# Linear and sliding-window attention in turn: a fourth slot of probabilities, the last tile by head halves, folded first values, and far masks on two engines

## The chip, the cores and the metric

The kernel runs on one core of a Trainium2 chip. The metric is the device time of one execution in microseconds; of the kernel before, three runs gave a median of 434.49 (433.9 to 435.25). The profile was taken on an execution whose span is 432.7 us. Engine names below: PE is TensorE's matmul, PEld its weight load, ACT is ScalarE, DVE is VectorE, POOL is GpSimd, SP is the queue that issues DMAs.

## The reference

Four residual layers on x of 2048 tokens by 512 features, 32 heads of 16: linear attention (A), causal attention in a window of 256 tokens (B), then A and B again with the same weights.

```python
def _A_ref(x, wqkv, wo):                       # linear attention
    q, k, v = split_heads(x @ wqkv)
    phi = lambda t: jnp.where(t > 0, t + 1, jnp.exp(t)) + 1e-6
    pq, pk = phi(q), phi(k)
    kv = jnp.einsum("bhsd,bhse->bhde", pk, v)
    z = jnp.einsum("bhsd->bhd", pk)
    num = jnp.einsum("bhqd,bhde->bhqe", pq, kv)
    den = jnp.einsum("bhqd,bhd->bhq", pq, z)[..., None] + 1e-6
    return merge_heads(num / den) @ wo

def _B_ref(x, wqkv, wo):                       # window W = 256
    q, k, v = split_heads(x @ wqkv)
    scores = jnp.einsum("bhqd,bhkd->bhqk", q, k) * (Dh ** -0.5)
    mask = (idx[:, None] - idx[None, :] >= 0) & (idx[:, None] - idx[None, :] < W)
    p = _softmax(jnp.where(mask[None, None], scores, -1e9), axis=-1)
    return merge_heads(jnp.einsum("bhqk,bhkd->bhqd", p, v)) @ wo

x = x + _A_ref(_layernorm(x), A_wqkv, A_wo)
x = x + _B_ref(_layernorm(x), B_wqkv, B_wo)
x = x + _A_ref(_layernorm(x), A_wqkv, A_wo)
x = x + _B_ref(_layernorm(x), B_wqkv, B_wo)
```

`split_heads` and `merge_heads` stand for the reshapes and transposes of the original.

## The kernel before

The program is written as a list of operations with their reads, writes and PSUM tiles. A table stored in the file fixes beforehand the order of all operations, the engine of those that may go to either ACT or DVE, and the PSUM bank of every tile; semaphores follow from that. Tokens lie in 16 tiles of 128. Excerpts, with cuts marked by `...`; the comments are added here.

```python
# loads, on SP: x in pieces between the first layer's weights
seq += [xs(0, 1), xs(1, 2), xs(2, 4), w("wAk", ...), xs(4, 6), w("wAv", ...)]
seq += [xs(6, 8), w("wAq", ...), xs(8, 12), xs(12, 16)]
...
# layer A: keys, values, queries of a tile; x is normalised and transposed first
def a_k(self, t, key):
    ps = self.tok("k", t, xT, lambda c: K.wA[:, c, 512:1024], ...)     # 4 matmuls, 128x512
    self.phi(ps, lambda: K.pk[:, t, :], ...)        # exp on ACT, min+add and max on DVE
def a_v(self, t, key):
    ps = self.tok("v", t, xT, lambda c: K.wA[:, c, 1024:1536], ...)    # 4 matmuls, 128x512
    self.copy("ve", ps, lambda: K.vA[:, t, :], ...)                    # ACT or DVE
def a_q(self, t, key):
    ps = self.feat("q", t, ...)                                        # 16 matmuls, 128x128
    self.phi(ps, lambda: K.XQ[:, :, t * P:(t + 1) * P], ...)
def a_kv(self, t, kv, z, key):                      # summed over the 16 tiles
    for f in range(4):
        e.matmul(K.ps(kv)[:, fs], K.vA[:, t, fs], K.pk[:, t, fs], ...)
    for f in range(4):
        m = e.matmul(K.ps(z)[:, f:f + 1], K.pk[:, t, fs], K.ones[:, 0:1], ...)
...
# between the keys and the output of a layer A: block mask, product with wo, denominators
self.on("DVE", "kvm", ... K.pqd[:, 0], K.ps(kv), K.bmask ...)
self.pe("M", ... K.pqd[:, 0, f, :], K.wAo[:, f, :] ...); self.copy("Me", ...)
self.pe("den", ...); self.on("DVE", "rec", ... e.reciprocal(K.recf[:], K.ps(ps)[:, 0:P]) ...)
...
def a_out(self, t, key):
    for f in range(4):                              # reciprocals spread over the features
        m = e.matmul(K.ps(ps)[:, f * P:(f + 1) * P], K.spread[:, tg, f, :], K.rec[:, G, :], ...)
    self.on("DVE", "pqd", ... K.pqd[:, s], K.ps(ps), K.XQ[...], ALU.mult ...)
    po = self.tok("aout", t, lambda f: K.pqd[:, s, f, :], lambda f: K.M[:, f, :], ...)
    self.resid(t, po, key + 0.15)
```

Layer B of a tile j of keys: the queries of the next 256 tokens are scored against 64-key blocks b, in four row groups of the array; ACT takes the exponentials into one of three slots of `pb`; DVE multiplies the triangles of the near part (`mk` in b_scores) and of the far part (`mk` in b_far) with a 0/1 mask; the value products of tile j read the slots of tiles j, j-1 and j-2.

```python
def b_scores(self, j, f, key):
    for b in range(2):
        for gq in range(4):
            m = e.matmul(K.ps(ps[gq])[:, 256 * b:256 * b + ns[b]], K.kB[rows, j % 4, 2 * f + b, :, :], K.XQ[rows, f, q:q + ns[b]], ..., tile_position=(32 * gq, 0))
    sl = j % 3
    for h in range(2):
        for b in parts:          # one ACTIVATE of 2x2x256, or two where the window is cut short
            self.on("ACT", "ex", ...)
    self.on("DVE", "mk", ... x, x, K.tri[:, 0, :] ..., ALU.mult ...)       # 128x512
def b_far(self, j, key):
    ...                          # 32 matmuls of 64 columns
    for h in range(2):
        for b in range(2):
            self.on("ACT", "ex", ...)                                      # 128x512
    for b in range(2):
        self.on("DVE", "mk", ... x, x, K.tri[:, 1, :] ..., ALU.mult ...)   # 128x1024
def b_values(self, j, h, key):
    m = e.matmul(K.ps(ps)[:, 34 * u:34 * u + 34], K.pb[:, (b // 2) % 3, gq, f, o:o + P], K.vB[:, (b // 2) % 4, b % 2, r, :], ...)
def b_out(self, j, key, by_pe):
    self.transpose("oT", ...)    # by DMA, of the last tile by PE and one copy
    po = self.tok("bout", j, ...); self.resid(j, po, key + 0.05)
```

The helpers give many operations one line: L351 is `tok` (four matmuls of 512 columns), L365 `feat` (eight of 128 columns), L340 `copy`, L535 and L573 the score matmuls, L549 and L550 the near exponentials (whole and cut), L583 the far ones, L556 and L590 the two masks, L608 the value products, L316 the normalisation, L284 the constant `spread`.

Of the kernel before, what the change touches and what calls it, by code (L numbers as in the profile page):

```python
# [8 lines left out]
ACT = mybir.ActivationFunctionType  # L9
# [14 lines left out]
    same=0.0, pe_first1=5, lat_t=4300, cap_s=8, cap_d=2, cap_e=6, mode=100, sem=35, ring_x=3, wait_s=200,  # L24
# [174 lines left out]


# [5 lines left out]
class Plan:  # L206
# [33 lines left out]
    def load(self, name, emit, nbytes, wr, key):  # L240
        ns = max(500, nbytes / 310)
        return self.on("SP", name, emit, key, (ns, ns + 2400), wr=wr)

    def setup(self):
# [10 lines left out]
        seq += [xs(0, 1), xs(1, 2), xs(2, 4), w("wAk", "wA", "A_wqkv", 512, 1024), xs(4, 6), w("wAv", "wA", "A_wqkv", 1024, 1536)]  # L255
        seq += [xs(6, 8), w("wAq", "wA", "A_wqkv", 0, 512), xs(8, 12), xs(12, 16)]
        seq += [w("wAo", "wAo", "A_wo", 0, 512), w("wBn", "nat", "B_wqkv", 0, 1024)]
        for i, (n, f, b, r) in enumerate(seq):
            self.load(n, f, b, r, key + i if n[0] == "x" or n[:3] in ("wAk", "wAv", "wAq") else 104 + 0.01 * i)
        i = len(seq)  # L260
        self.load("wBv", lambda e: e.dma_start(K.wBv[:], K.B_wqkv.rearrange("(k p) c -> p k c", p=P)[:, :, 1024:1536]), 524288, [("wBv",)], 106)
        self.load("wBo", lambda e: e.dma_start(K.wBo[:], K.B_wo.rearrange("(k p) c -> p k c", p=P)), 524288, [("wBo",)], 107)
# [11 lines left out]

        pool("c3", zero(lambda: K.bmask, 1.0), 151, 200, wr=[("bmask",)])
# [6 lines left out]
        pool("c9", zero(lambda: K.spread), 157, 2000, wr=[("spread",)])  # L282
        for tg in range(4):
            pool("c10", lambda e, tg=tg: e.affine_select(out=K.spread[:, tg, :, :], in_=K.spread[:, tg, :, :], compare_op=ALU.not_equal, fill=1.0, base=-32 * tg, pattern=[[-8, 4], [-1, 8], [0, 16]], channel_multiplier=1), 158, 700, rd=[("spread",)], wr=[("spread",)])  # L284
# [5 lines left out]
        sel = lambda i, base, pat, cm: (lambda e: e.affine_select(out=K.tri[:, i, :], in_=K.tri[:, i, :], compare_op=ALU.is_ge, fill=0.0, base=base, pattern=pat, channel_multiplier=cm))  # L290
        pool("c15", sel(0, 0, [[1, 64]], -1), 162, 200, rd=[("tri",)], wr=[("tri",)])
        pool("c15", sel(1, 64, [[1, 64]], -1), 162, 200, rd=[("tri",)], wr=[("tri",)])
        pool("c15", sel(1, -64, [[0, 64]], 1), 162, 200, rd=[("tri",)], wr=[("tri",)])
        self.on("DVE", "c16", lambda e: e.tensor_tensor(K.tri[:, 0, :], K.tri[:, 0, :], K.tri[:, 1, :], ALU.add), 12, (120, 200), rd=[("tri",)], wr=[("tri",)])
        self.on("DVE", "c16", lambda e: e.tensor_scalar(K.tri[:, 1, :], K.tri[:, 0, :], -1.0, 1.0, op0=ALU.mult, op1=ALU.add), 12, (120, 200), rd=[("tri",)], wr=[("tri",)])
# [13 lines left out]
    def norm(self, t, key, xn_slot, out, wr, by_pe):  # L309

        K = self
        self.on("DVE", "stats", lambda e: e.bn_stats(K.stats[:, t, :], K.xres[:, t, :]), key, dve(512), rd=[("xres", t)], wr=[("stats", t)])  # L312
        self.on("DVE", "aggr", lambda e: e.bn_aggr(K.mv[:, t, :], K.stats[:, t, :]), key + 0.01, (66, 150), rd=[("stats", t)], wr=[("mv", t)])  # L313
        self.on("POOL", "eps", lambda e: e.tensor_scalar(K.ve[:, t, :], K.mv[:, t, 1:2], LN_EPS, None, op0=ALU.add), key + 0.02, (300, 330), rd=[("mv", t)], wr=[("ve", t)])  # L314
        self.on("POOL", "pow", lambda e: e.tensor_tensor(K.rs[:, t, :], K.ve[:, t, :], K.negh[:], ALU.pow), key + 0.03, (640, 690), rd=[("ve", t), ("negh",)], wr=[("rs", t)])  # L315
        self.on("DVE", "xn", lambda e: e.tensor_scalar(K.xn[:, xn_slot, :], K.xres[:, t, :], K.mv[:, t, 0:1], K.rs[:, t, :], op0=ALU.subtract, op1=ALU.mult), key + 0.04, dve(512, "ptr"), rd=[("xres", t), ("mv", t), ("rs", t)], wr=[("xn", xn_slot)])  # L316
        self.transpose("T", lambda: K.xn[:, xn_slot, :], out, [("xn", xn_slot)], wr, key + 0.05, by_pe)
# [66 lines left out]
    def a_v(self, t, key):  # L384
        K = self
        xT = lambda c: K.XQ[:, c, t * P:(t + 1) * P]
        ps = self.tok("v", t, xT, lambda c: K.wA[:, c, 1024:1536], [("XQ", t), ("wAv",)], key)
        self.copy("ve", ps, lambda: K.vA[:, t, :], lambda: K.ps(ps), key + 0.1, 512, wr=[("vA", t)])
# [21 lines left out]
    def layer_a_keys(self, ph, base):  # L410
        self.cls = "E"
        for t in range(T):
            k = 100 * ph + t
            self.norm(t, k - 0.5, t % self.par["ring_x"], lambda t=t: self.XQ[:, :, t * P:(t + 1) * P], [("XQ", t)], t < self.par["pe_first1"])
            self.a_k(t, k)
            self.a_v(t, k + 0.05)
            self.a_q(t, 200 + 4 * (t // 4) + 0.2 * (t % 4) - self.par["k_aq2"])

    def barrier(self, ph):
# [3 lines left out]
        kv, z = Tile(1, "K", False), Tile(1, "K", False)  # L423
        key = 100 * ph + 16
        for t in range(T):
            self.a_kv(t, kv, z, 100 * ph + self.par["k_akv"] + t * 0.001 if late else 100 * ph + t + 0.6)
        key += 2
        if late:
            for t in range(T):
                self.a_q(t, 300 + 4 * (t // 4) + 0.2 * (t % 4) - self.par["k_aq3"])  # L430
        self.on("DVE", "kvm", lambda e: e.tensor_tensor(K.pqd[:, 0, :, :], K.ps(kv).rearrange("p (f n) -> p f n", f=4), K.bmask[:].unsqueeze(1).to_broadcast([P, 4, P]), ALU.mult), key - 2, dve(512), rd=[("bmask",)], wr=[("pqd", 0)], ps=[kv])
        self.on("DVE", "zs", lambda e: e.tensor_tensor(K.zs[:], K.hot[:], K.ps(z)[:, 0:4].unsqueeze(2).to_broadcast([P, 4, 32]), ALU.mult), key - 2, dve(128), rd=[("hot",)], wr=[("zs",)], ps=[z])
        for f in range(4):
            ps = Tile(1, K.cls)
            self.pe("M", lambda e, f=f, ps=ps: e.matmul(K.ps(ps), K.pqd[:, 0, f, :], K.wAo[:, f, :], start=True, stop=True), key - 2 + f * 0.01, 1, 512, rd=[("pqd", 0), ("wAo",)], ps=[ps])
            self.copy("Me", ps, lambda f=f: K.M[:, f, :], lambda ps=ps: K.ps(ps), key - 2 + f * 0.01, 512, wr=[("M", f)])
        for G in range(4):
# [18 lines left out]
            self.g.add("recb", {"ACT": act(128), "DVE": dve(128, "2x")}, lambda e, eng, G=G: e.activation(K.rec[:, G, :], K.recf[:], ACT.Copy) if eng == "ACT" else e.tensor_copy(K.rec[:, G, :], K.recf[:]), k + 0.1, rd=[("recf",)], wr=[("rec", G)])  # L456


    def a_out(self, t, key):
        K = self  # L460
        G, tg = divmod(t, 4)
        ps = Tile(1, K.cls)

        def put(e):
            m = None
            for f in range(4):
                m = e.matmul(K.ps(ps)[:, f * P:(f + 1) * P], K.spread[:, tg, f, :], K.rec[:, G, :], start=True, stop=True)
            return m

        self.pe("spread", put, key, 4, 128, rd=[("rec", G), ("spread",)], ps=[ps])  # L470
        s = t % 2
        self.on("DVE", "pqd", lambda e: e.tensor_tensor(K.pqd[:, s, :, :], K.ps(ps).rearrange("p (f n) -> p f n", f=4), K.XQ[:, :, t * P:(t + 1) * P], ALU.mult), key + 0.05, dve(512), rd=[("XQ", t)], wr=[("pqd", s)], ps=[ps])  # L472
# [404 lines left out]
```

The softmax here doesn't subtract the row's maximum and nothing guards it: scores larger than these inputs give would overflow.

## Time and profile before

| what | value |
|---|---|
| time, median of 3 | 434.49 us |
| span of the profiled execution | 432.7 us |
| PE busy | 402.1 us, 93% |
| DVE busy | 374.7 us, 87% |
| ACT busy | 355.3 us, 82% |
| POOL busy | 83.3 us, 19% |
| near exponentials L549 | 224 of 128x1024, 1050 ns each on average |
| far exponentials L583 | 112 of 128x512, 642 ns |
| far masks L590 | 56 of 128x1024, 678 ns |
| near masks L556 | 128 of 128x512, 415 ns |
| first score of the first layer B | 73.0 us |
| last score of the last layer B | 423.6 us |

Busy time is the union of an engine's instructions, each from its start to its end. Neighbours on one engine overlap, so the mean duration of an instruction is more than the distance from one to the next; for the rate of a stream, read the distance between starts, or a merged piece of the chain divided by its count. PE's ends are modelled, so PE always looks fuller than it is.

### The profile page before, as it was taken

What the parts mean: (1) busy time and instruction counts of PE and PEld (TensorE: products, weight loads), DVE (VectorE), ACT (ScalarE), POOL (GpSimd) and SP (SyncE); (2) the same over time, 40 slices, a digit from 0 to 9 for tenths busy, and PEclk for the clock granted to TensorE, in tenths of its full rate; (3) what the DMA queues carried; (4) which work ended last, traced back from release to release, by engine and by line L of the source; (5) the groups of instructions that cost most, each with busy time, mean ns of one, the idle gap of its engine ahead of it and who ended that gap; (6) DMA issues with size and microseconds to landing.
All of it is one profiled execution on the core that took longest, in us unless ns stands there. A gap on an engine that the chain in (4) does not pass through costs nothing.

```text
span 432.7 us, 17332 instructions
## 1 busy us (share of the span) xinstructions
PE 402.1 (93%) x7576; PEld 265.4 (61%) x7576; DVE 374.7 (87%) x838; ACT 355.3 (82%) x525; POOL 83.3 (19%) x177
## 2 busy tenths in 40 slices
PE   1999999999999999999999999999999999999675
PEld 0555777655665665655656778765667576666443
DVE  5997799999999999988988679999899898987545
ACT  1454546999999999999998443799999999999982
POOL 7789112011120111111000141111000101000000
PEclk9999999999999999999999999999999999999869
DMA  7635104424443555545421000234344443436321
GB/s 241 220 64 148 49 2 106 97 65 97 117 84 82 78 102 101 89 78 107 97 53 26 15 3 2 88 102 102 91 105 94 105 102 101 90 100 101 92 53 51
DMA packets 69292, 37.84 MB, mean 87 GB/s; under 512 B 49248, under 2 KB 64608, under 8 KB 69216
## 3 DMA queue, kind: packets, MB, share of 16 engines
q1 hardware_dynamic: 69216, 36.73, 36.9%
q8 instruction: 60, 0.98, 1.0%
q14 instruction: 16, 0.13, 0.1%
HBM read 6.29 MB, written 2.10 MB: 19 GB/s over the span
## 4 chain that ended last, share of the span: by engine, by line
PE 43%; ACT 41%; DVE 9%; DMA 3%; issue 1%; POOL 1%; SPq 1%; POOLq 0%
ACT pb L549 31%; PE ps L351 19%; PE ps L365 10%; ACT pb L583 7%; PE ps L608 6%; PE ps L535 3%; DMA xres<-in_A_x_dram 2%; ACT pb L550 2%; PE ps L402 1%; DVE stats L312 1%; ACT tE L374 1%; DVE xres L478 1%; DMA xT<-xn 1%; DVE xn L316 1%; PE ps L573 1%
## 5 line engine op out<-in xcount | busy, mean ns | idle before, releaser
L549 ACT ACTIVATE pb<-ps 128x1024 bf16<-128x1024 f32 x224 | 211.1, 1050 | 3.7 <-PE ps L535 2.7
L608 PEld LDWEIGHTS ps<-vB,pb 128*128 128x128 bf16 x2880 | 80.3, 96 | 16.8 <-issue 3.9
L608 PE MATMUL ps<-vB,pb 128*128 128x34 bf16 x2880 | 86.8, 178 | 2.0 <-ACT pb L549 1.0
L314 POOL TENSOR_SCALAR ve<-mv 128x1 f32<-128x1 f32 x64 | 18.1, 283 | 285.3 <-DVE mv L313 284.1
L351 PE MATMUL ps<-wA,XQ 128*128 128x512 bf16 x256 | 65.9, 387 | 3.2 <-DMA wA<-in_A_wqkv_dram 2.8
L365 PE MATMUL ps<-xT,wBp 128*128 128x128 bf16 x1024 | 66.9, 219 | 1.6 <-DVE o L620 0.5
L374 ACT ACTIVATE tE<-ps 128x512 bf16<-128x512 f32 x64 | 38.1, 605 | 35.6 <-PE ps L351 16.9
L365 PEld LDWEIGHTS ps<-xT,wBp 128*128 128x128 bf16 x1024 | 58.2, 98 | 9.5 <-issue 1.7
L583 ACT ACTIVATE pb<-ps 128x512 bf16<-128x512 f32 x112 | 60.8, 642 | 1.6 <-PE ps L573 1.2
L556 DVE TENSOR_TENSOR pb<-pb,tri 128x512 bf16<-128x512 bf16 x128 | 52.2, 415 | 8.6 <-ACT pb L550 4.3
L535 PE MATMUL ps<-XQ,kB 32*128 32x256 bf16 (+3 forms) x1024 | 49.9, 270 | 8.4 <-ACT pb L550 2.6
L478 DVE TENSOR_TENSOR xres<-ps,xres 128x512 bf16<-128x512 f32 x64 | 43.7, 684 | 5.9 <-PE ps L351 5.4
L312 DVE BATCH_NORM_STATS2 stats<-xres 128x6 f32<-128x512 bf16 x64 | 43.6, 686 | 5.5 <-DMA xres<-in_A_x_dram 4.8
L590 DVE TENSOR_TENSOR pb<-pb,tri 128x1024 bf16<-128x1024 bf16 x56 | 37.5, 678 | 1.3 <-ACT pb L583 1.3
L315 POOL TENSOR_TENSOR rs<-ve,negh 128x1 f32<-128x1 f32 x64 | 37.6, 587 | 5.3
L535 PEld LDWEIGHTS ps<-XQ,kB 32*128 32x128 bf16 x1024 | 15.3, 92 | 37.7 <-ACT pb L549 17.9
L351 PEld LDWEIGHTS ps<-wA,XQ 128*128 128x128 bf16 x256 | 21.7, 98 | 26.4 <-issue 4.9
L351 PE MATMUL ps<-wBo,oT 128*128 128x512 bf16 x128 | 35.2, 388 | 1.3 <-DVE oT L335 0.5
L365 PE MATMUL ps<-XQ,wA 128*128 128x128 bf16 x512 | 35.5, 219 | 0.0
L351 PE MATMUL ps<-M,pqd 128*128 128x512 bf16 x128 | 34.6, 380 | 0.5 <-DVE pqd L472 0.5
L365 PEld LDWEIGHTS ps<-XQ,wA 128*128 128x128 bf16 x512 | 30.9, 98 | 6.6 <-issue 0.4
L351 PE MATMUL ps<-wBv,xT 128*128 128x512 bf16 x128 | 33.9, 381 | 0.7 <-DVE vA L495 0.4
(77 smaller groups left out, 453.7 us busy)
## 6 DMA issues: line engine op xcount, KB each, us to landing
vB<-vA SPq DMA_DIRECT2D x128, 68.0 KB, 2.1
kB<-vA SPq DMA_DIRECT2D x64, 128.0 KB, 2.1
out_dram<-xres SPq DMA_DIRECT2D x16, 128.0 KB, 2.5
wA<-in_A_wqkv_dram SPq DMA_DIRECT2D x3, 512.0 KB, 9.4
xres<-in_A_x_dram SPq DMA_DIRECT2D x2, 512.0 KB, 8.1
pb<-in_B_wqkv_dram SPq DMA_DIRECT2D x1, 1024.0 KB, 9.6
xres<-in_A_x_dram SPq DMA_DIRECT2D x3, 256.0 KB, 3.8
wBv<-in_B_wqkv_dram SPq DMA_DIRECT2D x1, 512.0 KB, 4.3
```

Source lines behind the costliest of these rows:

```text
L312: self.on("DVE", "stats", lambda e: e.bn_stats(K.stats[:, t, :], K.xres[:, t, :]), key, dve(512), rd=[("xres", t)], wr=[("stats", t)])
L315: self.on("POOL", "pow", lambda e: e.tensor_tensor(K.rs[:, t, :], K.ve[:, t, :], K.negh[:], ALU.pow), key + 0.03, (640, 690), rd=[("ve", t ...
L351: m = e.matmul(K.ps(ps), lhs(c), rhs(c), start=c == 0, stop=c == 3)
L365: m = e.matmul(K.ps(ps)[:, f * P:(f + 1) * P], w(c, f), xT(c), start=c == 0, stop=c == 3)
L374: self.on("ACT", "E", lambda e: e.activation(K.tE[:, s, :], K.ps(ps), ACT.Exp, bias=0.0), key, act(512), wr=[("tE", s)], ps=[ps])
L478: self.on("DVE", "res", lambda e: e.tensor_tensor(K.xres[:, t, :], K.ps(po), K.xres[:, t, :], ALU.add), key, dve(512), rd=[("xres", t)], w ...
L535: m = e.matmul(K.ps(ps[gq])[:, 256 * b:256 * b + ns[b]], K.kB[rows, j % 4, 2 * f + b, :, :], K.XQ[rows, f, q:q + ns[b]], start=True, stop= ...
L549: return e.activation(x, bank().rearrange("p g (b n) -> p g b n", b=2), ACT.Exp, bias=0.0, scale=0.25)
L556: return e.tensor_tensor(x, x, K.tri[:, 0, :].unsqueeze(1).unsqueeze(1).to_broadcast([P, 4, 2, 64]), ALU.mult)
L583: return e.activation(K.pb[:, sl, 2 * h:2 * h + 2, :, o:o + 64], i, ACT.Exp, bias=0.0, scale=0.25)
L590: return e.tensor_tensor(x, x, K.tri[:, 1, :].unsqueeze(1).to_broadcast([P, 16, 64]), ALU.mult)
L608: m = e.matmul(K.ps(ps)[:, 34 * u:34 * u + 34], K.pb[:, (b // 2) % 3, gq, f, o:o + P], K.vB[:, (b // 2) % 4, b % 2, r, :], start=i == 0, s ...
```

## The change

All of it is one new program with a new stored table, so that every engine's order is new throughout. Its parts:

- Loads: keys' weights of the first layer before the queries' and values'; each load after the first five waits until an earlier one has landed. Most constants on POOL are made after the third tile's norm. Nine matmuls on a zeroed buffer go ahead of PE's first work.
- First layer: values are no longer computed. PE sums xn^T phi(k) over the tiles in four PSUM banks (`g`), four copies bring it to SBUF (`ge`), and 16 matmuls with the value weights give the same kv (`gv`). The sums z are made four tiles at a time.
- Both layers A: the spread of the reciprocals runs in four row tiles of the array at once for four tokens' tiles, and the products with it are written over the queries.
- Layers B: scores are grouped by block b and a pair of feature groups f, so that also the cut windows of tiles 14 and 15 take one ACTIVATE per group; two far exponentials of 128x512 become one of 128x1024; keys are interleaved, so that one triangle serves both halves; the far mask may be an affine_select on POOL or the multiply on DVE, as the table says (31 of 56 on POOL).
- Last layer: probabilities have a fourth slot, in memory that held the second layer A's values and keys. The last tile is transposed, copied, projected, added and stored by halves.
- Second layer A: values of tiles 5 to 15 are computed while the layer before is still running.

```diff
-        seq += [xs(0, 1), xs(1, 2), xs(2, 4), w("wAk", ...), xs(4, 6), w("wAv", ...)]
-        seq += [xs(6, 8), w("wAq", ...), xs(8, 12), xs(12, 16)]
+        seq += [xs(0, 1), xs(1, 2), w("wAk", ...), xs(2, 4), xs(4, 6), w("wAq", ...), xs(6, 8), xs(8, 12)]
+        seq += [xs(12, 16), w("wAv", ...), w("wAo", ...), w("wBn", ...)]
...
+            if t == 2:
+                self.consts([self.pow])
             self.a_k(t, k)
-            self.a_v(t, k + 0.05)
+            for h in range(2):
+                    for c in (2 * h, 2 * h + 1):
+                        m = e.matmul(K.ps(acc[c]), xn(t)[:, c * P:(c + 1) * P], K.pk[:, t, :], start=t == 0, stop=t == T - 1)
...
+        for c in range(4):
+            self.copy("ge", acc[c], lambda c=c: G(c), lambda c=c: K.ps(acc[c]), ...)
+        for f in range(4):
+                for c in range(4):
+                    m = e.matmul(K.ps(kv)[:, f * P:(f + 1) * P], K.wA[:, c, 1024 + f * P:1024 + f * P + P], G(c)[:, f * P:(f + 1) * P], ...)
...
+                for f in range(4):
+                    for tg in range(4):
+                        rows = slice(32 * tg, 32 * tg + 32)
+                        m = e.matmul(K.ps(bc[tg])[:, f * P:(f + 1) * P], K.spread[rows, f, :], K.rec[rows, G, :], ..., tile_position=(32 * tg, 0))
...
+                self.on("DVE", "pqd", ... x(), K.ps(b), x(), ALU.mult ...)     # x is XQ of a tile
...
-        sl = j % 3
+        sl = j % self.rp                               # rp: 3, in the last layer 4
...
-    def b_scores(self, j, f, key):
+    def b_scores(self, j, b, fs, key):                 # fs: a pair of f
...
-            for b in range(2):
-                    return e.activation(K.pb[:, sl, 2 * h:2 * h + 2, :, o:o + 64], i, ACT.Exp, ...)
+            def ex(e, h=h):
+                return e.activation(far(h), i, ACT.Exp, ...)                  # 128x1024
...
+                if eng == "POOL":
+                    return e.affine_select(out=x, in_=x, compare_op=ALU.is_ge, fill=0.0, base=-2, pattern=[[0, 16], [-2, 64]], channel_multiplier=1)
                 return e.tensor_tensor(x, x, K.tri[:, 1, :].unsqueeze(1).to_broadcast([P, 16, 64]), ALU.mult)
...
+            if last and j == T - 1:
+                self.b_last(j, k)
+                continue
             self.b_out(j, k, tail)
...
+                if j >= LATE:                          # LATE = 5
+                    self.a_v(j, base + par["k_av"] + 0.01 * j)
...
+                if name == "PE":
+                    e.wait_ge(wsem, 1)
+                    for _ in range(9):
+                        e.matmul(self.PS[:, 7, :], warm[:, 0:P], warm, start=True, stop=True)
```

## The prediction

> **What bounds the kernel now.** I read the page first: busy time by engine and the forty slices.
>
> ```profile
> PE 402.1 (93%) x7576; PEld 265.4 (61%) x7576; DVE 374.7 (87%) x838; ACT 355.3 (82%) x525; POOL 83.3 (19%) x177
> PE   1999999999999999999999999999999999999675
> DVE  5997799999999999988988679999899898987545
> ACT  1454546999999999999998443799999999999982
> ```
>
> No engine is the bound over the whole span: ACT has two full stretches with holes around them, PE is full where ACT is not, and at the end PE starves. So I cut the span where L535 (the scores of the sliding layers) begins and ends, and asked for the busy time of each stretch. Columns after the stretch: its length, then busy us of PE, PEld, DVE, ACT and POOL.
>
> ```profile
> 0.00:73.00 73.00, 62.93 (x672) 40.96 (x672) 62.08 (x139) 32.72 (x59) 39.91 (x83) 1.00 0.44 116
> 73.00:238.10 165.10, 159.96 (x3198) 101.78 (x3200) 153.32 (x351) 159.04 (x227) 22.22 (x52) 1.00 0.42 86
> 238.10:276.30 38.20, 37.93 (x626) 30.15 (x624) 30.94 (x68) 17.52 (x35) 9.06 (x18) 1.00 0.06 18
> 276.30:423.70 147.40, 136.21 (x2979) 89.18 (x2980) 124.22 (x273) 144.50 (x199) 12.14 (x25) 0.97 0.40 94
> 423.70:432.70 9.00, 5.04 (x116) 3.37 (x116) 4.17 (x10) 1.48 (x7) 0.00 (x0) 0.94 0.20 59
> ```
>
> Five stages, called A to E below. A (first linear layer): PE and DVE, with a slow start. B (first sliding layer): ACT is idle for 6.1 of 165.1 us, with PE and DVE close behind. C (second linear layer's barrier): PE, idle for 0.3 us. D (last sliding layer): ACT, idle for 2.9 us; PE and DVE have room. E: the drain after the last score. A saving counts only if it falls on the engine that its stage is short of.
>
> The start of stage A, from the timeline of PE:
>
> ```profile
> 9.31 1.86 PE L351 MATMUL ps<-wA,XQ 128*128 128x512 bf16 x4 [2.81 <-DMA wA<-in_A_wqkv_dram]
> 10.97 1.49 PE L328 MATMUL ps<-ident,xn 128*128 128x128 bf16 x12
> 12.36 1.89 PE L351 MATMUL ps<-wA,XQ 128*128 128x512 bf16 x4
> ...
> 15.06 6.24 PE L351 MATMUL ps<-wA,XQ 128*128 128x512 bf16 x28 [0.39 <-DVE pk L376]
> ```
>
> PE waits for weights until 9.31; then four 512-column matmuls take from 9.31 to 10.97, 1.66 us, where at 6.24/28 = 0.223 us each they need 0.89. The first matmuls run at about half speed although PEclk reads 1.00.
>
> The end of stage D, from the chain of work that ended last:
>
> ```profile
> 410.02 0.50 ACT pb L550
> ...
> 411.09 1.03 PE ps L351 x2
> 412.12 1.36 PE ps L608 x48
> 413.48 0.85 PE ps L351 x2
> 414.33 0.43 PE ps L535 x8
> ...
> 414.79 4.97 ACT pb L550 x11
> ```
>
> Here the chain leaves ACT for 3.7 us of PE work: tile 15's first exponentials write slot 15 mod 3 = 0, which tile 12 holds until the value products of tile 14 (L608) have read its far part.
>
> And one look at GpSimd beside VectorE, since the change gives GpSimd far more work:
>
> ```profile
> 12.15 1.07 DVE L316 TENSOR_SCALAR xn<-xres,mv,rs 128x512 bf16<-128x512 bf16 x1
> 12.22 0.85 POOL L284 TENSOR_SCALAR_AFFINE_SELECT spread<-spread 128x512 bf16<-128x512 bf16 x1
> ```
>
> L316 has a median of 406 ns; beside an affine_select of 852 ns it took 1.07 us and ended right after it.
>
> [...]For the mask multiply (two SBUF inputs) beside a long GpSimd read this trace has no clear case. [...]eight 256-column score matmuls start 0.32 us ahead of the next work (276.31 to 276.63) instead of 8 x 0.11, so four do run at once. [...]in the chain L583 with 512 elements comes every 0.49 us (four in 1.96), L549 with 1024 every 0.93 (eight in 7.44), so pairing two 512s saves only 0.05.
>
> **The change part by part.** Counts are from the instruction lists of both programs, put into stages by the order of issue; durations are spacings in the chain: 0.055 us for a 128-column matmul, 0.223 for a 512-column one, 0.025 for one of L608, 0.60 for a 512-element VectorE operation that reads PSUM (mean 685 ns, overlapped), 0.55 for such a copy on ACT.
>
> *Start.* The first key weights now share the queues with fewer later loads, and most GpSimd constants come after the first three norms. 1.3 MB land before the keys can start; at the 303 GB/s of 5 to 10 us that is 4.3 us, plus about 2.9 to issue and land (first x tile seen at 2.87): about 7.2 instead of 9.3, -2. [...]Cold work was two times (1.66 - 0.89), 12 transposes at 1.39 - 0.66 and some more: about -2.3.
>
> *Folded values.* The first layer's x W_v is replaced by (xn^T phi(k))^T W_v: 64 matmuls of 512 columns go and 64 come, so nothing there; 64 matmuls of 128 columns shrink to 16: 48 x 0.055 = -2.6 us of PE. Sixteen evacuations go, four come: 12 x 0.6 = -7 us over ACT and DVE. In return the barrier grows by a step: four copies (ACT alone, 2.2 us), 16 matmuls (0.9) before the block mask. q projections can fill most; I charge +2.
>
> *Spread by row tiles.* 128 full matmuls (0.89 per four tiles) become eight groups of about 0.33: -4.5 us of PE in all, of which A gets 0.5, C about as much and the rest lies in B and D where PE has room.
>
> *Stage A together*: -2 - 2.3 (start) - 2.6 - 0.5 - 1.8 (two q and two bq groups moved to B) + 2 = -7.2, and VectorE, at 62 of 73 us, will not let all of it through: **-6**.
>
> *Stage B.* ACT: far exponentials 14 x (4 x 0.49 - 2 x 0.93) = -1.4; the edge tiles 14 and 15, now by pairs of f: 8 x (0.50 + 0.40 + 0.27 + 0.16) = 10.6 down to 4 x (0.93 + 0.72 + 0.50 + 0.27) = 9.7, -0.9. Other ACT copies balance. DVE: 17 of 28 far masks go to GpSimd, 17 x 0.60 = -10. On GpSimd a 128x512 affine_select takes 0.85, 128x128 about 0.33, so 1.36 ns an element: an estimate of 1.55 us for 1024. If each blocks VectorE for half of that, 17 x 0.78 = +13. So VectorE gains nothing here by my count. **-3**.
>
> *Stage C.* q groups 21 to 13 (8 x 8 x 0.055 = -3.5, they move to D), v -1.3, spread -0.6, other small groups +2.4 (two bv, one pv, two bout), on a full PE: **-2.7**.
>
> *Stage D.* ACT: -1.4 and -0.9 as in B; the fourth slot takes the 1.4 us that ACT waits for L535 between 405 and 426 (the waits of ACT there). But ACT also gets 4 more exponentials of q (4 x 0.55), two key copies, one query copy and one value copy, and one small one: +4.6. Sum +0.9, call it **+1**: the fourth slot is mostly eaten by work that comes over from C.
>
> *Stage E.* Tile 15 by halves shortens transposes, copy and residual by about 0.2, 0.2 and 0.3, but tile 14's output product now ends after tile 15's: **-1**.
>
> Sum: -6 - 3 - 2.7 + 1 - 1 = -11.7; 434.5 - 11.7 = 422.8. Stage B's ACT idle time (6.1 us) may shrink too with the far masks off VectorE's queue and 1.5 us more come out of it; I say **421.5 us**.
>
> **The rivals.** [...]31 far masks x 1.55 = 48 us of GpSimd, each able to hold up VectorE's mask multiply, normalisation or minimum, and through VectorE the PSUM banks that PE and ACT need. For it: the 1.07 us above. Against: ACT bounds B and D, and D has 23 us of VectorE idle. If every mask blocked fully and B took a third of it, +8: 429. *Barrier wait in place of work*: the folded chain copies, product, mask, M is exposed; DVE and PE then idle in A as PE frees up: 425. *ACT in D only*: the fourth slot moves nothing and D grows by 3: 424. *Better overlap*: all of A's 7.2, B's 6.1 of ACT idle halved, D -2: 413.
>
> **Range and chances.** Most rivals cost 2 to 8 us, the good one gives 8; 8 in 10 between 412.0 and 430.0. The line of 2% is at 425.8, 4 us above my number: faster 0.77, same 0.20, slower 0.03.
>
> **What would show it.** Right: the first score at about 67 instead of 73.0; PE's first 512-column matmuls at 0.22 us; far exponentials near 1.03 us each for 1024 elements; no stretch of PE alone in the chain between the edge exponentials; the barrier's stretch near 35. Wrong: affine_select on pb far over 1.55 us, or VectorE's mask multiply rising from 415 ns beside it; ACT idle in B above 6 us; more than 3 us of PE idle around the fold; first score still at 71 or later.

## The result and the profile after

The changed kernel takes 437.83 us (median of four runs, 436.85 to 438.1) against 434.19 for the kernel before on the same chip: ratio 1.0079, 95% interval 1.0050 to 1.0107. The prediction said 421.5 us, with 430.0 as the upper end of its range. The profiled span is 436.0 us (before 432.7). Of the new orders below, the one at 435.5 us had two of its fourteen runs in a slower state, which are left out.

First the page of the changed kernel: busy time, then the slices of PE, DVE and ACT.

```profile
PE 392.6 (90%) x7460; PEld 257.6 (59%) x7539; DVE 358.8 (82%) x799; ACT 349.0 (80%) x434; POOL 115.7 (27%) x204
PE   6889999998988899989989999999889889998776
DVE  5879598989998899788888789988799589877464
ACT  2523447999799988989998444899999999999992
```

DVE has 15.9 us less to do and ACT 6.3. PE's 9.5 us less can't be taken as it stands: the page has 7460 matmuls (PE) for 7539 weight loads (PEld), so 79 records of matmuls are missing. The variant below whose loads don't wait for each other runs the same operations, and its page has them all:

```profile
PE 404.6 (92%) x7539; PEld 257.6 (59%) x7539; DVE 360.8 (82%) x799; ACT 349.1 (80%) x434; POOL 116.2 (27%) x204
```

About 4 us of that are the matmuls on zeros, so by this trace PE's own work is only some 1.5 us below the 402.1 of before. The time went up although two engines have less to do. Cut at the near scores (L593 now, L535 before) into the five stages of the prediction; after the stretch come its length and the busy us of PE, PEld, DVE, ACT and POOL:

```profile
0.00:71.60 71.60, 61.99 (x607) 35.99 (x621) 56.76 (x133) 28.72 (x50) 38.62 (x82) 0.98 0.45 122
71.60:241.50 169.90, 156.37 (x3158) 99.88 (x3190) 149.64 (x330) 156.84 (x186) 41.64 (x69) 1.00 0.35 81
241.50:277.20 35.70, 34.33 (x578) 26.32 (x582) 31.01 (x70) 16.04 (x29) 7.95 (x15) 1.00 0.09 24
277.20:426.70 149.50, 134.76 (x3026) 91.73 (x3052) 117.20 (x258) 145.72 (x167) 27.45 (x38) 0.96 0.38 93
426.70:436.00 9.30, 5.12 (x117) 3.64 (x116) 4.23 (x11) 1.68 (x5) 0.00 (x0) 0.87 0.19 45
```

| stage | before | after | difference | predicted |
|---|---|---|---|---|
| A | 73.0 | 71.6 | -1.4 | -6 |
| B | 165.1 | 169.9 | +4.8 | -3 |
| C | 38.2 | 35.7 | -2.5 | -2.7 |
| D | 147.4 | 149.5 | +2.1 | +1 |
| E | 9.0 | 9.3 | +0.3 | -1 |

B is where the forecast turned. There ACT's busy time fell by 2.2 us, as predicted, and DVE's by 3.7; but idle time rose for ACT from 6.1 to 13.1 us and for DVE from 11.8 to 20.3. PE's line for B lacks 32 matmuls. In the complete traces of the three variants of the start below, whose B has the same operations, PE is busy for 160.1 to 160.5 us and idle for 9.0 to 10.6, where before it was busy for 160.0 and idle for 5.1: its work in B did not shrink. What ACT waits for in B, first before, then after (total us, times, longest):

```profile
ACT pb L549 <- PE ps L535: 1.8, 5, 0.6
```

```profile
ACT pb L603 <- PE ps L593: 8.0, 14, 1.0
```

Most of what ACT waits for in B is scores: 8.0 us in 14 short waits, none above 1.0 us. PE's own waits in B are spread just as thin. There is no single long wait to point at; the experiments have to find the cause.

The start of A after the change, from PE's timeline:

```profile
1.24 3.92 PE L908 MATMUL ps<-kB 128*128 128x512 bf16 x9 [1.24 <-DVE kB L903]
5.63 0.40 PE L341 MATMUL ps<-ident,vp 128*128 128x128 bf16 x4 [0.47 <-DVE vp L329]
...
8.89 1.86 PE L364 MATMUL ps<-wA,XQ 128*128 128x512 bf16 x4 [1.88 <-DMA wA<-in_A_wqkv_dram]
...
12.90 1.03 PE L364 MATMUL ps<-wA,XQ 128*128 128x512 bf16 x4
```

The nine matmuls on zeros run, but between 5.2 and 8.9 us PE does little (two groups of four transposes), and the first keys take 1.86 us, as in the kernel before; the third group of keys takes 1.03. The granted clock was 0.50 from 8.89 to 11.00 us and 1.00 from 12.2 on; in the kernel before it was 1.00 beside the same 1.86. The key weights land at 8.89 instead of 9.31, far from the 7.2 I had worked out.

The end of D, in the chain of work that ended last:

```profile
413.48 0.44 DVE pb L609
...
413.97 1.48 PE ps L668 x48
...
416.31 1.48 PE ps L364 x3
417.79 0.50 PE ps L626 x30
...
418.32 1.02 ACT pb L635
...
432.24 0.42 DVE xres L720
432.66 0.67 DVE xres L532
```

The stretch in which the chain leaves ACT is still there, from 413.5 to 418.3. Tile 15 no longer waits for a slot; now the far scores (L626) come late, because PE's order puts value products and an output product ahead of them. ACT itself waits for scores for 1.2 us between 405 and 427, 0.4 of it here, where before the change it waited for 1.4. The last two lines are stage E: the halved residual of tile 15 (L720) is done at 432.66, and then the whole residual of tile 14 (L532) ends the program.

And the far mask on GpSimd beside VectorE, by tile (count: shortest/median/longest ns):

```profile
L609 DVE TENSOR_TENSOR pb<-pb,tri x112: 360/417/1200, 76.8 to 423.5; 128x512 bf16<-128x512 bf16 x112
L643 POOL TENSOR_SCALAR_AFFINE_SELECT pb<-pb x27: 1144/1145/1708, 102.5 to 389.9; 128x1024 bf16<-128x1024 bf16 x27
```

The affine_select takes 1145 ns, not the 1.55 us that I estimated. Six of the near masks shown (L609) overlap one; they average 706 ns, the longest 1200, where the others have a median of 417. So it is with the normalisation (L329: six beside one average 911 ns, median of the others 404), the minimum (L388: three at 944, against 288) and VectorE's own far masks (L644: five at 1000, against 683); the residuals, which read PSUM, show nothing (L532: six at 685, against 685). Summed over every VectorE operation that overlaps one of the 31 far masks, the excess over its own undisturbed median is 8.4 us, 6.7 of it in B and 1.7 in D.

### The profile page after: what moved, and what is told of

Read it like the earlier page. It is cut to its first block, busy times and chain, and to the rows that moved or that the text cites. A ratio compares the mean times of both kernels' runs of the same rounds, so it can differ in the third digit from the quotient of the medians.

```text
span 436.0 us, 17118 instructions
## 1 busy us (share of the span) xinstructions
PE 392.6 (90%) x7460; PEld 257.6 (59%) x7539; DVE 358.8 (82%) x799; ACT 349.0 (80%) x434; POOL 115.7 (27%) x204
## 4 chain that ended last, share of the span: by engine, by line
PE 42%; ACT 25%; DVE 19%; DMA 9%; issue 3%; POOL 1%; SPq 0%; DVEq 0%; ACTq 0%; POOLq 0%
ACT pb L603 16%; PE ps L364 15%; PE ps L378 9%; PE ps L668 8%; PE ps L593 4%; ACT pb L635 4%; ACT vp L603 3%; DMA xT<-xn 3%; DVE XQ L521 3%; DVE xres L532 2%; DMA XQ<-vp 2%; DVE stats L325 2%; DMA oT<-o 2%; DVE tE L388 2%; ACT tE L387 2%
## 5 line engine op out<-in xcount | busy, mean ns | idle before, releaser
L603 ACT ACTIVATE pb<-ps 128x1024 bf16<-128x1024 f32 (+2 forms) x224 | 207.0, 1021 | 10.5 <-PE ps L593 9.6
L593 PE MATMUL ps<-XQ,kB 32*128 32x256 bf16 (+2 forms) x1024 | 50.5, 272 | 7.7 <-ACT pb L603 3.1
L364 PE MATMUL ps<-wA,XQ 128*128 128x512 bf16 x176 | 48.3, 387 | 7.4 <-DMA XQ<-vp 2.4
L532 DVE TENSOR_TENSOR xres<-ps,xres 128x512 bf16<-128x512 f32 x63 | 43.0, 684 | 13.6 <-PE ps L364 13.3
L609 DVE TENSOR_TENSOR pb<-pb,tri 128x512 bf16<-128x512 bf16 x112 | 47.1, 431 | 8.0 <-ACT pb L603 7.4
L635 ACT ACTIVATE pb<-ps 128x1024 bf16<-128x1024 f32 x50 | 49.3, 1054 | 2.2 <-PE ps L626 2.1
L643 POOL TENSOR_SCALAR_AFFINE_SELECT pb<-pb 128x1024 bf16<-128x1024 bf16 x27 | 32.1, 1188 | 52.1 <-ACT pb L635 51.1
L593 PEld LDWEIGHTS ps<-XQ,kB 32*128 32x128 bf16 x1024 | 15.5, 93 | 36.3 <-ACT pb L603 14.6
L364 PE MATMUL ps<-wBo,oT 128*128 128x512 bf16 x104 | 30.6, 394 | 4.8 <-DMA oT<-o 1.4
L364 PE MATMUL ps<-M,XQ 128*128 128x512 bf16 x114 | 31.4, 380 | 3.4 <-DVE XQ L521 1.5
L364 PE MATMUL ps<-wBv,xT 128*128 128x512 bf16 x106 | 30.5, 381 | 2.7 <-issue 0.8
L364 PEld LDWEIGHTS ps<-wA,XQ 128*128 128x128 bf16 x192 | 16.1, 99 | 24.9 <-issue 4.3
```

The source lines that it names most:

```text
L364: m = e.matmul(K.ps(ps), lhs(c), rhs(c), start=c == 0, stop=c == 3)
L532: self.on("DVE", "res", lambda e: e.tensor_tensor(K.xres[:, t, :], K.ps(po), K.xres[:, t, :], ALU.add), key, dve(512), rd=[("xres", t)], w ...
L593: m = e.matmul(K.ps(ps[gq])[:, ns * i:ns * i + ns], K.kB[rows, j % 4, 2 * f + b, :, :], K.XQ[rows, f, q:q + ns], start=True, stop=True, ti ...
L603: return e.activation(out(2 * h, 2, ns), i, ACT.Exp, bias=0.0, scale=0.25)
L609: return e.tensor_tensor(x, x, K.tri[:, 0, :].unsqueeze(1).unsqueeze(1).to_broadcast([P, 4, n, 64]), ALU.mult)
L635: return e.activation(far(h), i, ACT.Exp, bias=0.0, scale=0.25)
```

## The experiments

All ratios are to the kernel before, run beside each variant on the same chip, with 95% intervals; stage lengths are of one profiled execution each. My theory at first was order: the sums are right, but the new fixed order of issue fits badly. Rivals: masks on GpSimd that hold VectorE up (the first expectation of the next two runs and of the one that sends masks of the kernel before to GpSimd), the start, the fourth slot, and the cost of the new operations themselves.

**Single parts undone.** In the changed kernel, all 56 far masks on VectorE:

```diff
+        if o.name == "mf":
+            o.eng = "DVE"
```

> The changed kernel with all 56 far masks on VectorE; the order is kept. [...](GpSimd's 31 masks of 1.145 us hold VectorE up, 8.4 us in all by the trace, and through it PE and ACT): back to 433 or below, a ratio to before of 0.985 to 0.997. Order theory (the new order has no slack, whatever engine masks): 31 x 0.6 = 18.6 us more work for VectorE[...], so 438 to 442, a ratio of 1.01 to 1.02.

437.3 us, 1.0087 (1.0056 to 1.0118); B 168.7, D 151.8. B gains 1.2, D loses 2.3. That is between the two expectations. Moving the masks to VectorE does not win the loss back; but as it trades the 8.4 us of excess for some 18.6 us more of VectorE's own work, it does not show that the excess costs nothing. The same kernel with the far mask cut to one column of 64 (its output lacks that masking), each mask on its own engine:

```diff
-    x = bass_view(K.P(sl)[:, 0, 0, 384 * b + 256:384 * b + 320], [[704, 16], [1, 64]])
+    x = bass_view(K.P(sl)[:, 0, 0, 384 * b + 256:384 * b + 257], [[704, 16], [1, 1]])
```

> The changed kernel with each far mask cut to one column of 64 (leaves out the masking of the other 63), on the engines as before[...]. [...]at least 8 us less than the changed kernel, 430 or below (ratio 0.99 or less). Order theory: masks were not what ACT and PE waited for; 435 to 437 (ratio 1.00 to 1.006).

433.11 us, 0.9983 (0.9965 to 1.0001); B 165.5, D 147.9, A, C and E as they were. This too lies between the expectations. So the masks together cost the changed kernel 0.96% (1.0079 - 0.9983), some 4.2 us, nearly all of it in B and D: as much as the whole loss. That became the thread.

**Single parts put into the kernel before.** The fourth slot in the last layer alone, in the same order:

```diff
-        sl = j % 3
+        sl = j % self.rp          # 4 in the last layer; the memory is that of pk, wAo and tE
```

> The kernel before with a fourth slot in the last layer alone (in memory of the second linear layer's keys, wo weights and two exp buffers), order kept. If the fourth slot frees the wait of tile 15 seen at the end of the chain (3.7 us of PE between exponentials, of which ACT idled 1.4): 431 to 433, ratio 0.993 to 0.997. If the order of PE keeps the waits anyway: ratio 0.999 to 1.001.

434.22 us, 1.0018 (1.0006 to 1.0030), D 147.9. The slot alone gives nothing. In the trace of this run the chain of work that ended last still leaves ACT for PE, from 410.1 to 413.5 us: in a fixed order a buffer that is free earlier doesn't move the work of PE that stands ahead of the next scores. (The changed kernel with three slots was not tried; its stored order has dependencies in a circle then.) Next, half of the far masks of the kernel before as affine_select on GpSimd (mask values not the reference's):

```diff
-            self.on("DVE", "mk", mk, ...)
+            self.on("POOL" if b == 0 else "DVE", "mk", mk, ...)
```

> The kernel before with half of its far masks (28 of 56, those of the even block) as affine_select on GpSimd, order kept; the selected pattern is the changed kernel's, so the mask's values are not the reference's. [...]VectorE saves 28 x 0.6 = 17 us and loses 8 in waits that sit on the path: slower, 436 to 440 (ratio 1.005 to 1.015). If GpSimd is a free helper: 430 to 433 (ratio 0.99 to 0.998). If masks are off the path: within 0.3%.

437.09 us, 1.0087 (1.0065 to 1.0110); B +1.0, D +1.8. Masks that cost nothing on VectorE (shown below) cost 0.9% when half are sent to GpSimd in the old order. VectorE's operations that overlap one of the 28 are 7.0 us longer in sum than their undisturbed medians, 4.6 in B and 2.4 in D. Whether that or the later delivery (an affine_select of this shape takes 1145 ns in the trace of the changed kernel, the multiply 678 in that of the kernel before) is what costs was not separated.

**The start.** Three variants of the changed kernel: one matmul on zeros in place of nine; eight more after the second transpose; loads that don't wait for earlier ones.

```diff
-                    for _ in range(9):
+                    for _ in range(1):
```

> The changed kernel with one warming matmul instead of nine. If the nine are wasted because PE stands idle again from 5.2 to 8.9 us (two transposes apart)[...]: within 0.2% of the changed kernel, ratio to before 1.006 to 1.010. If they do warm the first keys: 1 to 2 us slower than the changed kernel, ratio 1.010 to 1.013.

438.05 us, 1.0099 (1.0062 to 1.0136); first keys at 9.26 and as slow (1.87 us), first near score at 70.2.

```diff
+                    if name == "PE" and seen == 3:
+                        for _ in range(8):
+                            e.matmul(self.PS[:, 0, :], warm[:, 0:P], warm, start=True, stop=True)
```

> The changed kernel with eight more matmuls on zeros after the second transpose, which fill PE's wait for the first key weights (7.0 to 8.9 us). [...]the first four key matmuls in 0.9 instead of 1.66 us, and the first score at most 1.5 us earlier; ratio to before 1.003 to 1.007. If stage A is then held by VectorE or later loads: ratio 1.006 to 1.010 although the matmuls are fast.

439.63 us, 1.0122 (1.0090 to 1.0153). It does what it should for the first keys, as PE's timeline shows:

```profile
7.46 1.89 PE L916 MATMUL ps<-kB 128*128 128x512 bf16 x8
9.19 1.03 PE L364 MATMUL ps<-wA,XQ 128*128 128x512 bf16 x4
```

The keys take 1.03 in place of 1.86 us, yet the first near score comes at 71.5, as in the changed kernel, and the whole is slower than either expectation had it.

```diff
-            ..., begun[i - 4:i - 3] if i >= 5 else [])
+            ..., [])
```

> The changed kernel with no load waiting for an earlier one (order of issue kept). If the throttle starves stage A (x tiles 6 to 15 are asked for only at 8.8 us or later, and PE waits 2.1 us for a transpose at 20.5): first score 1 to 3 us earlier, ratio 1.001 to 1.006. If the weights then share the queues and keys start later: first keys at 10 us or later, ratio 1.007 to 1.012.

438.52 us, 1.0097 (1.0065 to 1.0129); keys at 9.67, first near score at 72.8. Runs whose A is exactly that of the changed kernel put the first near score anywhere between 70.5 and 71.8, so of these three only the last stands clearly apart: what is won in the first 10 us is not seen at the end of A.

**New orders of the same operations.** Only the stored table is exchanged: issue order, the engine of either-or operations, PSUM banks.

> Exactly the operations of the changed kernel, their dependencies and its buffers, in another fixed order: the issue order, the engine of the operations that may run on either of two (18 far masks move from VectorE to GpSimd, 8 the other way, some twenty small evacuations change between ScalarE and VectorE) and the PSUM banks were searched anew with durations from the two traces. The median operation moves by 9 of 2596 places. ORDER theory (the operations are cheaper than before's, and the fixed order of the change is a bad fit to the chip: scores issued late, ScalarE left idle): clearly below both kernels, 418 to 428 us, ratio to the kernel before 0.96 to 0.985, with ScalarE's idle time in the second stage (170 us long after the change) back from 13 to under 8 us and the stage below 166 us. COST theory (the new operations cost more on the chip than their durations show: masks that block VectorE, strided key copies): no order helps much, 433 to 438 us, ratio 0.997 to 1.01.

432.93 us, 0.9992 (0.9972 to 1.0013).

> The same as the run before it, another order out of the same search (it ended 1.4 us worse by the durations it was searched with). It tells how far the time of one order can be told from those durations. ORDER theory: 419 to 429 us, within 3 us of the other. COST theory: 433 to 438 us. If the two differ by more than 4 us, an order's time hangs on something that the durations don't hold, and then the loss of the change can be of that kind too.

436.75 us, 1.0074 (1.0057 to 1.0091).

> The operations of the kernel before, untouched, in an order found by the same search with the same effort. It tells what of the gain of a new order belongs to the change's operations. ORDER theory, with cheaper operations in the change: 421 to 428 us, ratio 0.97 to 0.985, and 3 to 8 us above the changed kernel's operations in their own new order. COST theory: as good as the changed kernel's operations in their best order, or better.

435.14 us, 1.0035 (1.0019 to 1.0051). Against my expectation the search won little or nothing. A, B and D of the first re-planned order show how it goes wrong:

```profile
0.00:64.80 64.80, 58.60 (x586) 35.56 (x595) 55.71 (x131) 27.11 (x47) 37.58 (x81) 0.97 0.45 122
64.80:230.62 165.82, 155.32 (x3179) 102.48 (x3212) 149.37 (x336) 154.46 (x179) 46.48 (x72) 1.00 0.40 88
...
267.03:423.18 156.15, 136.24 (x3036) 91.20 (x3060) 118.98 (x256) 145.75 (x165) 37.03 (x48) 0.97 0.37 88
```

A is 6.8 us shorter than after the change, so the fold and the start do allow 65 us; B is 4.1 shorter, back at the 165.1 of before but no better; D is 6.6 longer, with ACT, busy as before, now idle for 10.4 us. Search once more, with delays added where PE changes between scores and other work (what the trace shows of them is in the last section) and with scattered transfer times:

> The operations of the changed kernel once more in a new order, this time searched with durations that were corrected after the first two re-planned orders gained far less than the search had promised:[...] every DMA takes one of four drawn times spread like those in the traces (transposes 2.4 to 4.5 us, copies of keys and values 1.9 to 4.0), so that an order with no slack for a late transfer counts as bad. By these durations the order is 8.4 us shorter than the change's own and 4.1 shorter than the first re-planned one. ORDER theory (the loss of the change lies in an order without slack for what its durations did not hold): 425 to 430 us, ratio 0.98 to 0.993, below both kernels. If it is within 2 us of the first re-planned order (431 to 435 us), the corrected durations still miss what sets the time, and order as the cause is shown only as far as three orders of the same operations differ. COST theory (operations cost more than their durations): 433 to 438 us.

435.5 us, 1.0019 (0.9995 to 1.0043).

> The operations of the kernel before in an order of the second search, with the same corrected durations; by them it is 8.6 us shorter than the order of the kernel before and 3 us longer than the changed kernel's operations in theirs. ORDER theory with somewhat cheaper operations in the change: 426 to 431 us, ratio 0.982 to 0.995, and 1 to 4 us above the re-planned changed kernel of the same call. COST theory: as fast as that one or faster.

437.82 us, 1.0081 (1.0058 to 1.0104). Order does matter: four orders of the changed operations run from 432.9 to 437.8 us, three of the old ones from 434 to 437.8. But in the sense of my theory, that a better order would show the new operations to be cheaper by several us, it fell. The second search promised 8.4 and 8.6 us; the chip gave 2.6 (1.0079 to 1.0019) and took 3.5.

**Masks and pairing.** Two facts remained: masks cost the changed kernel 1%, and its main saving for ACT is the far exponential of 1024 in place of two of 512. The kernel before with its far masks cut in the same way (output lacks that masking):

```diff
-    x = K.pb[:, sl, :, :, o:o + 64].rearrange("p g f n -> p (g f) n")
+    x = K.pb[:, sl, :, :, o:o + 1].rearrange("p g f n -> p (g f) n")
```

> The kernel before with its 56 far masks cut to one column of 64 (its output lacks that masking). The same cut took 4.7 us from the changed kernel. MASKS EXPOSED BY THE CHANGE: VectorE has slack in the kernel before and masks are hidden; ratio 0.995 to 1.002. MASKS COST THE SAME IN BOTH: ratio 0.985 to 0.993, and the masks are then no part of the loss.

434.14 us, 1.0006 (0.9993 to 1.0020). In the kernel before far masks are free. The same cut in the first re-planned order:

> The first re-planned order of the changed kernel, with its 56 far masks (41 of them on GpSimd) cut to one column of 64 (output lacks that masking). If masks cost the changed operations something in any order: 427 to 430 us, ratio 0.982 to 0.991. If their cost came with the change's own order: 431.5 to 434 us, ratio above 0.994.

430.84 us, 0.9930 (0.9902 to 0.9957): they cost that order 0.6%, between the two expectations. Then the pairing alone in the kernel before, each pair at the place of its later half:

```diff
-            for b in range(2):
-                def ex(e, h=h, b=b): ...                      # 128x512
-                self.on("ACT", "ex", ex, ..., act(512), wr=[("F", sl, h, b)], ...)
+            def ex(e, h=h): ...                               # 128x1024
+            self.on("ACT", "ex", ex, ..., act(1024), wr=[("F", sl, h, 0), ("F", sl, h, 1)], ...)
```

> The kernel before with one part of the change alone: two far exponentials of 128x512 become one of 128x1024 at the place of the later one, 56 in place of 112; the order of all else is kept, 7 masks excepted that move behind the exponential they now need. WORK theory (what ScalarE is spared in the two stages where it is full is gained): 28 x 2 x 0.05 = 2.8 us less, 431.0 to 432.5 us, ratio 0.992 to 0.997. GRAIN theory (a larger operation hands its PSUM banks back and its results on later, and that eats the saving): ratio 0.999 to 1.005.

437.70 us, 1.0084 (1.0066 to 1.0102); B +3.3, D +1.7. One part of the change, the one meant to spare ACT, costs as much as the whole change. B in this kernel:

```profile
71.88:240.30 168.42, 160.36 (x3202) 101.74 (x3200) 153.52 (x352) 157.78 (x199) 21.81 (x52) 1.00 0.40 84
```

ACT's work is 1.3 us less than before, and the stage is 3.3 longer. VectorE's wait for far exponentials before its far mask points to why; first the kernel before, then this one:

```profile
DVE pb L590 <- ACT pb L583: 1.3, 3, 0.5
```

```profile
DVE pb L591 <- ACT pb L584: 5.5, 8, 1.2
```

The first mask needed two exponentials of 512; now it needs both of 1024, and VectorE, whose order the table fixes, stands still for up to 1.2 us with other work behind the mask. If that is the way the cost takes, it should vanish when the masks are cut:

> The kernel before with paired far exponentials, and with its far masks cut to one column of 64 besides (output lacks that masking). If pairing costs through the far mask that waits for it (MASK QUEUE theory): the 3.8 us come back, 431 to 434.5 us, ratio 0.993 to 1.001. If pairing costs through PSUM banks that come free later or through the scores that ScalarE waits for (BANK theory): 436 to 438 us, ratio 1.005 to 1.009, as with full masks.

432.51 us, 0.9983 (0.9972 to 0.9994). The cost vanishes, but the wait does not:

```profile
DVE pb L591 <- ACT pb L584: 6.6, 8, 1.7
```

The cut masks still stand in line for the exponentials. What has changed is that they occupy VectorE for 11.5 us in place of 37.6, which leaves it time to catch up after a wait. The paired exponentials hold their PSUM banks in this run as in the last, so late banks are not the cost. Without the masks' time the pairing gains 0.23% (1.0006 to 0.9983), 1.0 us of the 2.8 expected. And the pairing undone in the changed kernel:

> The changed kernel with this part undone: each far exponential of 128x1024 becomes two of 128x512 in the same place, and a far mask waits only for the two that it needs. ScalarE gets 56 x 0.05 = 2.8 us more. If the pairing is what the change loses by in its own order too: 433 to 436 us, ratio 0.997 to 1.004. If the change's order has been made for the paired form, so that splitting only adds work and shifts every operation behind it: 440 to 447 us, ratio 1.013 to 1.03.

443.21 us, 1.0231 (1.0208 to 1.0255). Splitting is far worse there, as the second expectation had it: in that order it adds work and shifts what stands behind. So this run does not show that the pairing is what the changed kernel loses by. Last, the pairing in the kernel before with whole masks, and only the places of the 56 masks changed (34 stand later, 6 earlier, 16 as they were):

> The kernel before with paired far exponentials and whole far masks; against the run with the pairing alone nothing is changed but the place of the 56 far masks among VectorE's operations (found by a search that was allowed to move nothing else; the median mask moves 2 places later, a fourth of them 7 or more; all other operations keep their order). MASK QUEUE theory: the masks no longer stand in front of others while they wait, 431.5 to 434.5 us, ratio 0.995 to 1.001, with VectorE's wait for the far exponential back from 5.5 to under 2.5 us. If the place is not what costs: 436 to 438 us, ratio 1.005 to 1.009.

432.97 us, 0.9988 (0.9969 to 1.0007). VectorE's groups now show the far mask with hardly an idle moment ahead of it (count, busy us, mean ns, idle before):

```profile
L591 DVE TENSOR_TENSOR pb<-pb,tri 128x1024 bf16<-128x1024 bf16 x56 | 37.9, 678 | 0.3
```

B is 165.2 us again. The same work as in the run at 437.7; some 4 us (1.0084 - 0.9988 = 0.96%) were the place of these masks. It beats the changed kernel by 0.9%, but can't be told from the kernel before: none of these versions with whole masks clearly beats both.

Does the changed kernel lose by the same wait? Its trace speaks against it. Of its 56 far masks VectorE does 25; the line has the 23 on `pb`, and before the two on the fourth slot it has no idle time:

```profile
L644 DVE TENSOR_TENSOR pb<-pb,tri 128x1024 bf16<-128x1024 bf16 x23 | 16.8, 745 | 0.2 <-ACT pb L635 0.2
```

VectorE stands still ahead of them for 0.2 us in all, not for 5.5.

| | far masks whole | far masks cut |
|---|---|---|
| before | 1 | 1.0006 |
| before, far exponentials paired | 1.0084 | 0.9983 |
| the same, masks moved | 0.9988 | not run |
| changed | 1.0079 | 0.9983 |
| changed, first new order | 0.9992 | 0.9930 |

## Why the prediction was wrong

- **Stage B, -3: the failed step** was to count ACT's saving as gained time because ACT bounds B. The saving came (ACT busy -2.2, against 2.3 in the sum), but ACT's idle time rose from 6.1 to 13.1 us and B by 4.8. The prediction said of B that "PE has room"; in fact PE was idle for 5.1 us there, less than ACT, and its work did not shrink (160.0 before, 160.1 to 160.5 after). What the saving can do is shown in the kernel before: the pairing alone, in the old order, costs 0.84% because far masks then wait for the later, larger exponentials at the head of VectorE's queue; moving masks alone takes it back, and the wait of 5.5 us is gone with it.
- **What the changed kernel itself loses by** is shown only in part. Far masks that were free before (1.0006) cost it 0.96%, as much as the whole loss; without them B is 4.4 us and D 1.6 us shorter in the profiled runs. But the wait that explains the pairing is not there (0.2 us ahead of VectorE's far masks), so another way must carry the cost. That GpSimd's masks hold VectorE up is a rival that no run excludes: the excess on VectorE, 6.7 us in B and 1.7 in D, lies where the cut gains; so does that of the first new order (3.5 us in B and 7.0 in D, where the cut gains 0.4 and 3.8); and the run with all masks on VectorE exchanged it for more work. Another is the plain time of the masks on VectorE, if the new order leaves it no slack where they stand; this too was not tested.
- **The masks explain the rise, not the missing gain.** With them cut the changed kernel stands at 0.9983, not at the 0.97 that was forecast, and B at 165.5, no shorter than before. Of the 16.3 us between forecast and result, A is 4.6, B 7.8 (4.4 of them masks), C 0.2, D 1.1, E 1.3, and 1.3 is what the prediction took off besides for ACT's idle time in B, which grew instead.
- **VectorE held up by GpSimd's masks** was my first rival, and I had set the -10 us of masks moved off VectorE against +13 for it, so counted nothing. The +13 was an estimate: half of an estimated 1.55 us for each mask, on the strength of one pair in the trace (1.07 us for a normalisation with a median of 406 ns). The excess was smaller (6.7 us in B); but I never asked what a mask costs by its place, or what a slow mask on GpSimd delays.
- **Stage A, start, -2 and -2.3:** both terms failed. Keys came 0.4 us sooner, not 2, and after the pause the first four took 1.86 us, as before. That nine matmuls at the very start would speed them up was my assumption, and the trace of the kernel before did not show it; eight right ahead of the keys did (1.03 us). But that run shows the deeper error: it is 1.1 us ahead at the fifth group of transposes (13.55 in place of 14.64), and A ends where it did (71.5), though runs with one and the same A differ by 1.3 us there. Folding did take PE work away: in the complete trace of the run whose loads don't wait, A has 64.4 us of PE, 4.0 of them on zeros, against 62.9, so 2.6 less of PE's own work; that went into idle time there. The first new order, with 64.8, shows that a shorter A could be had, at the price of a longer D; I had not priced that.
- **Stage C, -2.7:** right (-2.5): PE was idle for 0.3 us there before, and its work fell by 2.8 (35.1 in the complete traces, from 37.9).
- **Stage D, +1:** +2.1. The fourth slot alone moves nothing; the step that gave it 1.4 us failed, since the freed wait was replaced by other late scores (1.2 us between 405 and 427).
- **Stage E, -1:** failed (+0.3): the halves of tile 15 end sooner, but tile 14's residual ends the program. The prediction named that and still took 1 us off.
- **Range:** the rivals were each taken from one base that had every saving in it. None was "ACT's work shrinks and its waits grow by more", and that is what happened in B. Of its own signs of being wrong these came: ACT idle in B above 6 us (13.1), the first score at 71 or later (71.6), near masks longer beside a select (706 in place of 417 ns).

Open: by which way the masks cost the changed kernel its 0.96% (the excess beside GpSimd, or the masks' own time on VectorE), and why the searched orders give 6 to 12 us less than measured durations promise.

## What to carry to other kernels

In a program with a fixed order on several nearly full engines, a saving on the engine that looks like the bound is not time yet: ask what the larger operation now hands over later, and which instruction stands first in line for it on another engine. When operations are merged, move their consumers back in the same step; in the kernel before, with its far exponentials merged, moving far masks was worth 1.0% (1.0084 to 0.9988). To test whether an operation is free, cut it to almost nothing in both kernels: "free before, 1% after" led to the masks where waits, spread over dozens of places, did not. Such a cut tells what an operation costs, not by which way: the wait for it can stay and only become harmless. And compare an engine's records with their partners, here matmuls with weight loads, before reading idle time from a trace.

## What the runs showed of the hardware

- PE loses time on both sides of the scores in four row tiles. In the trace of the kernel before, groups of scores that follow other work without a wait end a median of 114 ns later than their columns explain (120 groups, at the 216 ns that separate the ends of 512-column matmuls), and the work after them ends a median of 108 ns late (129 cases). What the delay is made of no run separates. By its weight loads the changed kernel changes between shapes of the array 333 times, the kernel before 313 times; eight of the new groups are the spread by row tiles.
- In the changed kernel PE ran 3.92 us of matmuls on zeros, then for 3.7 us only two short groups of transposes, and the first four 512-column matmuls of the keys took 1.86 us; with eight more on zeros right ahead of them they took 1.03. The four transposes in the pause took 0.40 us, against 0.61 after a single matmul on zeros; but in the run whose loads don't wait they took 0.61 although the nine ran there too.
- affine_select on GpSimd in the trace of the changed kernel: 1145 ns for 128x1024 in bf16, 850 ns for 128x512, so 0.58 ns an element (of one partition) between the two; my estimate had used 1.36.
